# Head pairs 6 and 7 move from plain float32 to float32r split stacks and channel-major numerators

## The chip, the cores and the metric

One core of one Trainium2 chip runs the whole program. The metric is the device time of one execution in microseconds (us). A profiled execution also gives a trace: start and duration of every instruction on the five engines (PE is TensorE's matmuls, PEld its weight loads, DVE VectorE, ACT ScalarE, POOL GpSimd; SP issues most transfers).

## The reference, cut to what matters

Two stages, chained. First a feature-map attention without softmax over 8 batches, 8 heads, 576 positions, head width 64, 128 features:

```python
def phi(x):
    proj = np.einsum('bhsd,df->bhsf', x, w_phi)
    proj = proj - np.max(np.abs(proj), axis=-1, keepdims=True)
    return np.concatenate([np.exp(proj), np.exp(-proj)], axis=-1)
q_p, k_p = (phi(q), phi(k))
kv = np.einsum('bhsf,bhsd->bhfd', k_p, v)
z = np.sum(k_p, axis=2)
num = np.einsum('bhsf,bhfd->bhsd', q_p, kv)
den = np.einsum('bhsf,bhf->bhs', q_p, z)[..., None] + 1e-06
x = num / den                       # heads side by side: (8, 576, 512)
```

Then a mixer over x: token mixing `u = x + (relu(x.T @ w_tok1) @ w_tok2).T` (576 to 256 and back), and channel mixing `u + relu(u @ w_ch1) @ w_ch2` (512 to 1536 and back).

## The kernel before

Heads are worked in pairs: pair i holds heads 2p and 2p+1 of batch i // 4, so there are 32 pairs, four to a batch. Five Python generators emit the work (`weave`, L635): `keys` (L280) and `queries` (L347) walk the pairs, `token_stream` the batches in two halves of two pairs each, `load_weights` the weights, `channel_stream` the 18 blocks of 256 positions. The framework then schedules the emitted instructions on each engine's queue by a timeline of its own; every engine runs its queue in order.

**Projection** (`less_max`, L218). A plain pair (i < `PLAIN`) is loaded by `load_plain` (L269), the keys of pair i in the upper 64 partitions and the queries of pair i in the lower 64, and multiplied by `wz` (w_phi padded with zeros) as float32, one 128x128 matmul for each 128 positions: 9 for the keys, 9 for the queries. The trace has two records for each plain float32 matmul. A split pair is loaded by `load` (L262) into `raw`, and `stack` (L206) writes a rounded copy by DVE (L213) and the remainder by POOL (L214) into the two halves of a tile; one float32r matmul 256 wide then gives two partial projections, which ACT copies (L246) and DVE adds (L248). In both, DVE takes the largest absolute value (L253); the subtraction of it (L255) is on DVE for a plain pair (it reads PSUM), on POOL for a split one. ACT makes the two exponentials (L299).

**Key-value sums** (`add_kv`, L310): 18 float32 matmuls a pair into `pkv`, with 128 moving columns for i < `ROWS` and 65 behind them. For i < `ROWS` ACT copies them out once (L333); behind, ACT rounds them (L341) and DVE makes the remainder (L343).

**Numerators.** The projected queries are transposed on PE (L393) and exponentiated. For i < `ROWS`, `row_numerators` (L418) has positions in rows: 20 float32 matmuls with 65 columns (L432, 40 records), a division on DVE (L445 to L447) into `rows`, 5 transposes back (`flip`, L451). Behind them `numerators` (L463) has channels in rows: ACT makes a rounded copy (L406), DVE and POOL the remainders (L407), and 24 float32r matmuls of 256 and 320 columns follow (`pn`), with DVE transposes of the denominators (L479, L484) and a product on POOL (L486).

**Token mixing** (`token_mix`, L500) takes `rows` as they are when the half has them; otherwise it transposes `xt` on PE (`px`, L510). The remainder of its input is on POOL with `rows`, on DVE without.

**Channel mixing** (`channel_mix`, L549): six up-projections `h` of 24 matmuls a block (`up_proj`), each followed by a ReLU on ACT (`gh`, L576) and a remainder on DVE (`gl`, L577), and six down-projections into `acc`. `h` has one PSUM buffer, so the next up-projection waits until `gl` has read it. The two weight matrices of this stage arrive as 64-bit floats and are converted on the core until some 155 us: ACT (L147), four DVE instructions on 128x512 elements (L148 to L151, `bitsc`), ACT's rounding and POOL's remainder (L75, L78, `wc`).

Of the kernel before, what the change touches and what calls it, by code (L numbers as in the profile page):

```python
# [22 lines left out]
T = 256  # L23
E = 1536
NC_, NE, NT = C // P, E // P, T // P
PLAIN = 8
ROWS = 8
BURST = 8
GATES = [1, 2, 2, 3, 4, 4, 5, 6, 6, 7, 7, 7]
HELD = {15: 1, 17: 2, 19: 3, 21: 4}  # L30
# [15 lines left out]
def mixer_kernel(ctx, tc, qk, vm, vt, w_phi, w1, w2, wc1, wc2d, out):  # L46
# [159 lines left out]
    def stack(raw, base, name):  # L206

        out = []
        lo = D - base
        for k, (c, n) in enumerate(((0, 512), (512, 640))):  # L210
            t = wk.tile([P, n], F32R, tag=f"{name[0]}{k}", name=f"st{name}{k}", bufs=1)
            src = raw[base:base + D, c:c + n]
            nc.vector.tensor_copy(t[base:base + D], src)  # L213
            nc.gpsimd.tensor_tensor(t[lo:lo + D], src, t[base:base + D].bitcast(F32), op=ALU.subtract)  # L214
            out.append(t)
        return out
# [45 lines left out]
    def load(i):  # L262

        raw = wk.tile([P, 2 * S], F32, tag="raw", name=f"raw{i}", bufs=1)
        lo, hi = (D if i <= PLAIN else 0), (D if i == B * NP else P)
        nc.sync.dma_start(raw[lo:hi], qk[i, lo:hi])
        raws[i] = raw

    def load_plain(i):  # L269

        out = []
        for k, (c, n) in enumerate(((0, 512), (512, 640))):
            t = wk.tile([P, n], F32, tag=f"{'kq'[i % 2]}{k}", name=f"pair{i}{k}", bufs=1)
            nc.sync.dma_start(t[D:], qk[i, D:, c:c + n])
            out.append(t)
        for k, (c, n) in enumerate(((0, 512), (512, 640))):
            nc.sync.dma_start(out[k][:D], qk[i + 1, :D, c:c + n])
        pairs[i] = out

    def keys():  # L280
        groups = [[(0, 0), (0, 1)], [(0, 2), (0, 3)], [(1, 0), (1, 1)], [(1, 2), (1, 3)], [None]]
        todo = None
        for i in range(B * NP):
            yield from until(lambda: i < 2 or i - 2 in asked)
            if i < PLAIN:
                load_plain(i)
# [4 lines left out]
            for j in range(2):  # L291
                queue.dma_start(v_sb[j * D:(j + 1) * D, 4, j, :D], vt[i, j])
            plain = D if i < PLAIN else None
            ts = pairs[i] if i < PLAIN else stack(raws[i], D, f"k{i}")
            for g, us in enumerate(groups):
# [14 lines left out]
    def add_kv(i, g, us, kp, v_sb):  # L310
# [4 lines left out]
        for n, u in enumerate(us):  # L315
            for sg in range(2):
                if u is None:
                    o, v = pkv[:, sg], v_sb[:, 4]
                elif i < ROWS:
                    c = (2 * u[1] + u[0]) * (D + 1)  # L320
# [7 lines left out]

        if i < ROWS:
            kv = wk.tile([P, 2, 4, D], F32, tag="kv0", name=f"kv0_{i}", bufs=1)  # L330
# [16 lines left out]
    def queries():  # L347
        turned, split_up, row_major = None, None, None
        pieces = [(i, k, j) for i in range(B * NP) for k in range(2) for j in range(2)] + [None] * 3
        for piece in pieces:  # L350
# [4 lines left out]
            if split_up:  # L355
                yield from until(lambda: split_up[0] in kvs)
                if split_up[0] < ROWS:
                    row_major = row_numerators(*split_up)
# [8 lines left out]
            if piece:  # L367
                i, k, j = piece
                if (k, j) == (0, 0):
                    plain = 0 if i < PLAIN else None  # L370
                    if i < PLAIN:
                        yield from until(lambda: i in pairs)
# [13 lines left out]
    def turn(i, k, j, pm, tail):  # L386
# [11 lines left out]
        for sg in range(2):  # L398
            full = wk.tile([P, SEG[0][1]], F32, tag="qf", name=f"qf{i}_{k}{j}{sg}")[:, :w]
            nc.scalar.activation(full, src, AF.Exp, scale=1.0 - 2.0 * sg)  # L400
            if i < ROWS:
                qps.append(full)
# [15 lines left out]
    def row_numerators(i, k, j, qps):  # L418

        b, p = divmod(i, NP)
        h, p = divmod(p, 2)
        n = 3 - k
        if j == 0:
            sums[0] = ps_w.tile([P, 2, 3, D + 1], F32, **REST, name=f"pr{i}_{k}")
        pn = sums[0]
        at = (D if j == 1 else 0) if k == 0 else 0
        for u in range(n):
            w, c = (P, at + u * P) if u < 2 else (D, 0 if j == 1 else 2 * P)  # L430
            for sg in range(2):
                nc.tensor.matmul(pn[:w, j, u], qps[sg][:, c:c + w], kvs[i][:, sg, j],  # L432
                                 start=j == 0 and u == 0 and sg == 0, stop=j == 1 and u == n - 1 and sg == 1,
                                 skip_group_check=True)
        if j == 0:
            return None
        if (b, h) not in rows_of:
            rows_of[b, h] = wk.tile([P, 5, 2 * P], F32, tag="rows", name=f"rows{b}_{h}")
        x = rows_of[b, h][:, 3 * k:3 * k + n, p * P:p * P + P].rearrange("p u (j d) -> p j u d", j=2)
        den = column(wk, 8, tag="dn", name=f"dn{i}_{k}", bufs=4)  # L440
        if i < NP:
            gates.append(den[:, :1])
        for w, a, e in ((P, 0, 2), (D, 2, 3))[:2 - k]:
            d = den[:w, 2 * a:2 * e].rearrange("p (j u) -> p j u", j=2)
            nc.vector.tensor_scalar(d, pn[:w, :, a:e, D], 1e-6, None, op0=ALU.add)  # L445
            nc.vector.reciprocal(d, d)
            nc.vector.tensor_tensor(x[:w, :, a:e], pn[:w, :, a:e, :D],  # L447
                                    d.unsqueeze(3).to_broadcast([w, 2, e - a, D]), op=ALU.mult)
        return i, k
# [40 lines left out]
    def until(cond):  # L490
        while not cond():
            yield None
# [205 lines left out]
```

## Time and profile before

| | us |
|---|---|
| median of 3 runs | 1130.9 (1129.98 to 1130.96) |
| the profiled execution | 1130.58 |
| its span, first to last instruction | 1128.8 |
| PE busy in it | 1109.2 |
| DVE, ACT, POOL busy | 669.1, 542.7, 512.0 |

The span is 1.8 us below the time of its own execution. The granted TensorE clock is 0.999 over the run, so 2.4 GHz. Matmul records overlap (each is some 280 ns long while one starts about every 117 ns), so what a matmul costs is read from the spacing in the chain of work, and not from its record's length.

### The profile page before, as it was taken

How to read it: one execution, taken by the hardware profiler on the slowest of the kernel's cores; microseconds unless marked ns; L12 is line 12 of the kernel's file. 1: busy time of each engine (PE TensorE's matmuls, PEld its weight loads, DVE VectorE, ACT ScalarE, POOL GpSimd, SP SyncE). 2: the span in 40 equal slices, each digit the busy share in tenths (PEclk: the TensorE clock that was granted, in tenths of full speed). 3: DMA queues.
4: the chain of work that ended last, by engine and by line, in shares of the span. 5: the costliest groups of instructions: out<-in, count | busy, mean ns of one | idle time of the engine just before them, and what ended most of it. 6: DMA issues, size and time to landing. Idle time of an engine off the chain costs nothing.

```text
span 1128.8 us, 24388 instructions
## 1 busy us (share of the span) xinstructions
PE 1109.2 (98%) x9280; PEld 1092.9 (97%) x9280; DVE 669.1 (59%) x1655; ACT 542.7 (48%) x1589; POOL 512.0 (45%) x675
## 2 busy tenths in 40 slices
PE   8999999999999999999999999999999999999998
PEld 7998999989999999989999999999999999999998
DVE  7889864476575756677465573664756675542111
ACT  5766543445464644556454463544645565441110
POOL 2334332465464744756364472644645474330110
PEclk9999999999999999999999999999999999999999
DMA  7545401111110111111011110111101110000000
GB/s 210 169 127 163 138 16 43 32 52 33 29 54 20 33 33 51 33 51 33 20 33 51 33 51 1 52 33 38 46 19 33 51 33 12 20 1 19 20 20 20
DMA packets 66164, 54.39 MB, mean 48 GB/s; under 512 B 44992, under 2 KB 56768, under 8 KB 66048
## 3 DMA queue, kind: packets, MB, share of 16 engines
q1 hardware_dynamic: 64528, 52.41, 15.9%
q8 instruction: 74, 1.21, 0.4%
q10 hardware_dynamic: 1520, 0.43, 0.2%
q14 instruction: 42, 0.34, 0.1%
HBM read 43.38 MB, written 9.44 MB: 47 GB/s over the span
## 4 chain that ended last, share of the span: by engine, by line
PE 87%; DVE 5%; POOL 3%; ACT 2%; DMA 2%; issue 1%; SPq 0%; POOLq 0%; ACTq 0%; DVEq 0%
PE acc L84 26%; PE h L84 26%; PE pkv L324 9%; PE pn L84 6%; PE ph L84 3%; PE pa L84 3%; PE pt L393 3%; PE pr L432 2%; PE ppk L239 2%; PE ppq L239 2%; PE px L510 1%; POOL stq L214 1%; PE ppq L243 1%; PE ppk L243 1%; DMA raw<-in_w 1%
## 5 line engine op out<-in xcount | busy, mean ns | idle before, releaser
L84 PE MATMUL acc<-gh,wc 128*128 128x256 f32 x1728 | 342.6, 283 | 0.2 <-ACT gh L576 0.2
L84 PEld LDWEIGHTS acc<-gh,wc 128*128 128x128 f32 x1728 | 275.6, 188 | 0.8 <-ACT gh L576 0.7
L84 PE MATMUL h<-uh,wc_h 128*128 128x256 f32 x864 | 245.5, 285 | 0.6 <-DVE gl L577 0.5
L84 PE MATMUL h<-uh,wc_l 128*128 128x256 f32 x864 | 244.4, 283 | 0.0
L84 PE MATMUL h<-ul,wc_h 128*128 128x256 f32 x864 | 243.6, 282 | 0.8 <-POOL ul L557 0.8
L84 PE MATMUL acc<-gl,wc 128*128 128x256 f32 x864 | 241.9, 282 | 0.0
L84 PEld LDWEIGHTS h<-uh,wc_h 128*128 128x128 f32 x864 | 162.5, 188 | 2.0 <-DVE gl L577 1.6
L84 PEld LDWEIGHTS h<-ul,wc_h 128*128 128x128 f32 x864 | 162.8, 188 | 1.2 <-POOL ul L557 1.1
L84 PEld LDWEIGHTS acc<-gl,wc 128*128 128x128 f32 x864 | 162.7, 188 | 0.0
L84 PEld LDWEIGHTS h<-uh,wc_l 128*128 128x128 f32 x864 | 162.5, 188 | 0.0
L324 PE MATMUL pkv<-v,kp 128*128 128x65 f32 (+2 forms) x1152 | 156.3, 270 | 0.6 <-ACT kv L333 0.2
L299 ACT ACTIVATE kp<-pmk 128x256 f32<-128x256 f32 (+1 forms) x320 | 109.6, 393 | 94.0 <-POOL pmk L255 76.7
L577 DVE SCALAR_TENSOR_TENSOR gl<-h,gh 128x512 fp32r<-128x512 f32 x108 | 74.4, 689 | 131.0 <-ACT gh L576 127.3
L407 POOL TENSOR_TENSOR ql<-qf,qh 128x320 fp32r<-128x320 f32 (+1 forms) x96 | 80.7, 840 | 152.7 <-ACT qh L406 146.7
L400 ACT ACTIVATE qf<-pt 128x320 f32<-128x320 f32 (+1 forms) x256 | 103.7, 417 | 94.4 <-PE pt L393 76.9
L324 PEld LDWEIGHTS pkv<-v,kp 128*128 128x128 f32 x1152 | 146.1, 191 | 2.3 <-ACT kp L299 1.2
L576 ACT ACTIVATE gh<-h 128x512 fp32r<-128x512 f32 x108 | 64.8, 600 | 131.6 <-PE h L84 130.3
L557 POOL TENSOR_TENSOR ul<-xt,uh 128x64 fp32r<-128x64 f32 (+3 forms) x120 | 60.5, 531 | 95.4 <-ACT uh L556 94.6
L84 PE MATMUL pn<-qh,kv 128*128 128x320 f32 (+1 forms) x384 | 101.0, 302 | 1.8 <-DVE xs L515 1.8
L255 POOL TENSOR_TENSOR pmk<-pk,mxk 128x256 f32<-128x256 f32 (+1 forms) x120 | 71.9, 599 | 43.7 <-DVE mxk L253 23.5
L255 POOL TENSOR_TENSOR pmq<-pq,mxq 128x256 f32<-128x256 f32 x96 | 61.6, 642 | 62.8 <-DVE mxq L253 57.6
L214 POOL TENSOR_TENSOR stq<-raw,stq 64x512 fp32r<-64x512 f32 (+1 forms) x48 | 69.7, 1452 | 37.9 <-DVE stq L213 35.3
(124 smaller groups left out, 2251.6 us busy)
## 6 DMA issues: line engine op xcount, KB each, us to landing
raw<-in_qk SPq DMA_DIRECT2D x23, 576.0 KB, 3.8
rawc<-in_wc SPq DMA_DIRECT2D x24, 512.0 KB, 4.1
v<-in_vm SPq DMA_DIRECT2D x31, 256.0 KB, 3.4
out_x<-xt SPq DMA_DIRECT2D x12, 256.0 KB, 2.2
out_x<-xt SPq DMA_DIRECT2D x16, 192.0 KB, 2.0
pair<-in_qk SPq DMA_DIRECT2D x16, 160.0 KB, 4.0
pair<-in_qk SPq DMA_DIRECT2D x16, 128.0 KB, 3.8
raw<-in_w SPq DMA_DIRECT2D x8, 256.0 KB, 5.9
```

Source lines behind the costliest of these rows:

```text
L84: nc.tensor.matmul(o, a, m, start=first and i == 0, stop=last and i == 2, skip_group_check=group_ok)
L214: nc.gpsimd.tensor_tensor(t[lo:lo + D], src, t[base:base + D].bitcast(F32), op=ALU.subtract)
L239: nc.tensor.matmul(ps[:, i].rearrange("p two f -> p (two f)"), t[:, c:c + P], wp2.rearrange("p two f -> p (two f)"), start=True, stop=True)
L255: eng.tensor_tensor(pm[:, :n], pr, mx[:, :n].unsqueeze(2).to_broadcast([P, n, F]), op=ALU.subtract)
L299: nc.scalar.activation(kp[:, :len(us), sg], pm[:, :len(us)], AF.Exp, scale=1.0 - 2.0 * sg)
L324: nc.tensor.matmul(o, kp[:, n, sg], v, start=g == 0 and n == 0 and sg == 0, stop=u is None, skip_group_check=True)
L393: nc.tensor.transpose(ptr[:, n], r, ident)
L400: nc.scalar.activation(full, src, AF.Exp, scale=1.0 - 2.0 * sg)
L407: (nc.gpsimd if sg else nc.vector).tensor_tensor(lo, full, hi.bitcast(F32), op=ALU.subtract)
L557: nc.gpsimd.tensor_tensor(l[:, d:d + n], t[:, c, o:o + n], h[:, d:d + n].bitcast(F32), op=ALU.subtract)
L576: nc.scalar.activation(gh, ph, AF.Relu)
L577: nc.vector.scalar_tensor_tensor(gl, ph, 0.0, gh.bitcast(F32), op0=ALU.max, op1=ALU.subtract)
```

## The change

Two constants. `PLAIN` decides which pairs are loaded and projected as plain float32, `ROWS` which have 128-column key-value sums and row-major numerators:

```diff
-PLAIN = 8
-ROWS = 8
+PLAIN = 6
+ROWS = 6
```

Pairs 6 and 7 are the second half of batch 1, so token mixing of that half takes the `px` transposes. The emitted order changes with it. Three places show how.

On PE, where the keys of pair 6 are projected (`ppk`; `pf` are the transposes back of pair 5, `pkv` its key-value sums, `h_0` channel mixing's first up-projection), a piece of the difference:

```order
 L84 MATMUL ph_1_1_1_1523<-w_h,al_1_1437 128x256
-L243 MATMUL ppk_0_1555<-wz,pair_1546 128x128 x2
+L84 MATMUL h_0_1589<-uh_2_1579,wc_h 128x256
+L239 MATMUL ppk_0_1557<-wp_89,stk_1551 128x256 x2
 L324 MATMUL pkv_1331<-v_111,kp_4_1503 128x2x65 x2
-L84 MATMUL h_0_1583<-ul_2_1574,wc_h 128x256
-L84 MATMUL h_0_1583<-uh_2_1573,wc_l 128x256
-L84 MATMUL h_0_1583<-uh_3_1577,wc_h 128x256
+L84 MATMUL h_0_1589<-ul_2_1580,wc_h 128x256
+L84 MATMUL h_0_1589<-uh_2_1579,wc_l 128x256
+L84 MATMUL h_0_1589<-uh_3_1583,wc_h 128x256
 L458 MATMUL pf_0_1467<-ident,rows_0_1406 128x128 x2
```

The projection keeps its place; two float32 matmuls (four records) became two float32r ones (two records).

On DVE, around the first remainder `gl_0` of channel mixing (`bitsc` are weight conversions, `rows` and `dn` the numerators of pair 4):

```order
+L248 TENSOR_TENSOR pk_0_1562<-ppk_0_1557,partk_0_1560 128x256
 L446 RECIPROCAL dn_0_1407<-dn_0_1407 64x2
-L255 TENSOR_TENSOR pmk_0_1560<-ppk_0_1555,mxk_0_1558 128x256
 L149 TENSOR_SCALAR bitsc_6_1372<-bitsc_6_1372 128x512
 L151 SCALAR_TENSOR_TENSOR bitsc_5_1339<-rawc_5_1337,bitsc_5_1339 128x512
+L253 TENSOR_REDUCE mxk_0_1564<-pk_0_1562 128x2
 L447 TENSOR_TENSOR rows_0_1406<-pr_0_1293,dn_0_1407 64x128
-L577 SCALAR_TENSOR_TENSOR gl_0_1609<-h_0_1583,gh_0_1608 128x512
 L150 SCALAR_TENSOR_TENSOR bitsc_6_1372<-rawc_6_1370,bitsc_6_1372 128x512
-L253 TENSOR_REDUCE mxk_1_1697<-ppk_1_1694 128x2
+L577 SCALAR_TENSOR_TENSOR gl_0_1615<-h_0_1589,gh_0_1614 128x512
```

The additions of pair 6 stand between the same conversions, its subtractions are gone from here, and the remainder stands one conversion later.

On POOL, in the same stretch (`stk_15..` is the stack of pair 6, `stk_2066` the first of pair 7, `wc` the weight remainders):

```order
 L78 TENSOR_TENSOR wc_l<-bitsc_1_512_1209,wc_h 128x512
+L214 TENSOR_TENSOR stk_1551<-raw_1546,stk_1551 64x512
 L78 TENSOR_TENSOR wc_l<-bitsc_2_512_1220,wc_h 128x512
 L78 TENSOR_TENSOR wc_l<-bitsc_3_512_1262,wc_h 128x512
-L557 TENSOR_TENSOR ul_2_1574<-xt_0_397,uh_2_1573 128x256
-L557 TENSOR_TENSOR ul_3_1578<-xt_0_397,uh_3_1577 128x256
+L557 TENSOR_TENSOR ul_2_1580<-xt_0_397,uh_2_1579 128x256
+L557 TENSOR_TENSOR ul_3_1584<-xt_0_397,uh_3_1583 128x256
+L214 TENSOR_TENSOR stk_1554<-raw_1546,stk_1554 64x640
 L78 TENSOR_TENSOR wc_4_1300<-bitsc_4_1303,wc_4_1300 128x512
+L255 TENSOR_TENSOR pmk_0_1566<-pk_0_1562,mxk_0_1564 128x256
 L78 TENSOR_TENSOR wc_5_1336<-bitsc_5_1339,wc_5_1336 128x512
```

The stack remainders and the subtractions of pair 6 now stand among the weight remainders.

## Rows read from the trace of the kernel before

**Rows 1.** The page: busy time, share of the span, instructions of each engine
```profile
PE 1109.2 (98%) x9280; PEld 1092.9 (97%) x9280; DVE 669.1 (59%) x1655; ACT 542.7 (48%) x1589; POOL 512.0 (45%) x675
```
**Rows 2.** Windows: length, busy us of PE, PEld, DVE, ACT, POOL, clock, DMA
```profile
82.00:121.00 39.00, 37.01 (x301) 34.85 (x301) 38.01 (x86) 23.99 (x57) 17.71 (x18) 1.00 0.51 151
121.00:156.00 35.00, 35.00 (x302) 34.35 (x303) 27.35 (x63) 19.21 (x47) 11.79 (x10) 1.00 0.26 87
82.00:151.00 69.00, 67.01 (x559) 64.39 (x560) 62.53 (x142) 40.63 (x95) 28.36 (x27) 1.00 0.42 129
```
**Rows 3.** Timeline of DVE and of PE: second and fifth remainder, next up-projection
```profile
120.24 0.68 DVE L577 SCALAR_TENSOR_TENSOR gl<-h,gh 128x512 fp32r<-128x512 f32 x1
120.98 0.39 PE L84 MATMUL h<-uh,wc_h 128*128 128x256 f32 x1
150.43 0.68 DVE L577 SCALAR_TENSOR_TENSOR gl<-h,gh 128x512 fp32r<-128x512 f32 x1
153.66 0.28 PE L84 MATMUL h<-uh,wc_h 128*128 128x256 f32 x1
```
**Rows 4.** The chain that ended last, in time: start, us, what, how many records
```profile
122.55 1.21 PE pr L432 x12
130.43 0.45 PE ppk L243 x4
131.33 0.89 PE pkv L324 x8
174.95 0.42 PE pf L458 x3
...
286.23 0.22 PE px L510 x2
430.77 0.88 PE pn L84 x6
439.62 0.47 PE pn L84 x4
```
**Rows 5.** Groups by shape, whole run: count, busy us, mean ns, idle before
```profile
L213 DVE CAST stk<-raw 64x640 fp32r<-64x640 f32 x24 | 14.3, 598 | 10.0 <-PE ppk L239 9.4
L213 DVE CAST stk<-raw 64x512 fp32r<-64x512 f32 x24 | 12.8, 534 | 12.2 <-DMA raw<-in_qk 8.8 <-PE ppk L239 2.8
L255 DVE TENSOR_TENSOR pmk<-ppk,mxk 128x256 f32<-128x256 f32 x32 | 13.1, 411 | 0.3
L214 POOL TENSOR_TENSOR stk<-raw,stk 64x640 fp32r<-64x640 f32 x24 | 37.4, 1558 | 16.3 <-DVE stk L213 16.0
L214 POOL TENSOR_TENSOR stk<-raw,stk 64x512 fp32r<-64x512 f32 x24 | 31.0, 1290 | 15.9 <-DVE stk L213 10.0 <-POOL ql L407 2.9 <-POOL pmq L255 1.7
L255 POOL TENSOR_TENSOR pmk<-pk,mxk 128x256 f32<-128x256 f32 x96 | 62.3, 649 | 39.9 <-DVE mxk L253 23.5 <-PE h L84 7.9 <-PE pkv L324 3.1
```
**Rows 6.** Timeline of DVE and of POOL: conversions alone and beside POOL
```profile
108.32 0.41 DVE L149 TENSOR_SCALAR bitsc<-bitsc 128x512 uint32<-128x512 uint32 x1
115.70 0.68 DVE L151 SCALAR_TENSOR_TENSOR bitsc<-rawc,bitsc 128x512 uint32<-128x512 uint32 x1
117.14 1.51 DVE L149 TENSOR_SCALAR bitsc<-bitsc 128x512 uint32<-128x512 uint32 x1
117.10 1.27 POOL L78 TENSOR_TENSOR wc<-bitsc,wc 128x512 fp32r<-128x512 f32 x1 [2.41 <-ACT wc L75]
```
**Rows 7.** Groups by shape of DVE, 82 to 121 us: count, busy us, mean ns
```profile
L151 DVE SCALAR_TENSOR_TENSOR bitsc<-rawc,bitsc 128x512 uint32<-128x512 uint32 x10 | 8.0, 802 | 0.1
L150 DVE SCALAR_TENSOR_TENSOR bitsc<-rawc,bitsc 128x512 uint32<-128x512 uint32 x10 | 7.8, 789 | 0.0
L149 DVE TENSOR_SCALAR bitsc<-bitsc 128x512 uint32<-128x512 uint32 x9 | 6.0, 671 | 0.1
L148 DVE TENSOR_SCALAR bitsc<-bitsc 128x512 f32<-128x512 f32 x9 | 5.2, 578 | 0.4 <-ACT bitsc L147 0.4
```
**Rows 8.** Window in which token mixing of batch 1 meets the next pairs
```profile
226.00:254.00 28.00, 26.10 (x204) 24.48 (x203) 20.15 (x48) 13.76 (x44) 17.29 (x21) 1.00 0.19 52
```

## The prediction

> **What bounds the kernel now.** I read the page first: PE is busy 98% of the span, no engine beside it and its weight loads over 59% [rows 1]. That is a mean, so I read windows next. From 82 to 121 us DVE is busy 38.0 of 39.0 us and PE 37.0; from 121 to 156 PE is busy all 35 us and DVE 27.4 [rows 2]. So there are two regimes: up to some 121 us DVE and PE are both full (DVE converts the channel weights there), behind it PE alone sets the pace and a matmul less is time less, if its inputs come in time. The timeline shows where one regime hands over: the second remainder of channel mixing ends on DVE at 120.9 us, and the up-projection that needs its PSUM buffer starts at 120.98; at the fifth the remainder ends at 151.1 and the sixth up-projection starts at 153.66, 2.6 us later [rows 3]. The pairs that change are worked just here, between 104 and some 220 us, half of them where DVE has no room.
>
> **What PE loses.** Prices are spacings in the chain [rows 4]; one plain float32 matmul is two records. Projections of a pair: before 18 matmuls, 36 records at 0.45/4 = 0.1125 us, 4.05 us; after 18 records of 256 columns, as the numerators' 256-column ones at 0.47/4 = 0.118, 2.12 us. Saved 1.93. Numerators: before 40 records at 1.21/12 = 0.101 and 5 transposes back at 0.42/3 = 0.14, together 4.74 us; after 12 of 320 columns at 0.88/6 = 0.147, 12 of 256 at 0.118 and 5 `px` transposes at 0.22/2 = 0.11, together 3.72. Saved 1.02. The key-value sums keep 36 records; 128 columns go at 0.89/8 = 0.111, the 65-column row I have nearest is the numerators' 0.101, so at most 0.36 us, and I count nothing, since both seem set by the weight load that each record has. Sum 2.95 us a pair, **5.9 us for two** (6.6 with the key-value sums).
>
> **What DVE gets before the hand-over.** I follow it to the fifth remainder, `gl_4`, and count in the order of both kernels. Ahead of it stand six casts for three stacks (keys of 6, queries of 6, keys of 7) and seven additions that are new, and nine subtractions that are gone. Casts 3 x (0.598 + 0.534) = 3.4 us; seven additions less nine subtractions, all at about 0.41, -0.8 [rows 5]. So 2.6 us more work of its own. The maximum stays.
>
> **What POOL adds, and what that does to DVE.** Ahead of the same point POOL gets six stack remainders, 3 x (1.558 + 1.290) = 8.5 us, and seven subtractions at 0.649, 4.5 us: 13.1 us [rows 5]. POOL has the time: 17.7 of 39.0 us before 121, 11.8 of 35 behind it [rows 2]. But it slows DVE: a conversion step that takes 0.41 us alone took 1.51 when a POOL subtraction of 1.27 us began 0.04 us ahead of it [rows 6]. The mean price: in 82 to 121 us the four steps average 0.578, 0.671, 0.789 and 0.802 [rows 7], against 0.41 for the first two and 0.68 for the others alone (I take the one step of each length that [rows 6] has), so 9 x 0.17 + 9 x 0.26 + 10 x 0.11 + 10 x 0.12 = 6.2 us lost, for 17.7 us of POOL: 0.35 us a POOL microsecond. The bounds are nothing (POOL works while DVE reads PSUM) and 1 (each POOL instruction blocks a step entirely). Of the 13.1 us, 5.4 stand ahead of the second remainder (two stack remainders of pair 6, one of pair 7, two subtractions): 1.9 us. For the other 7.7 I take two thirds of the price, since DVE is then busy 78% and not 97% [rows 2] and fewer conversions are left: 1.8 us. Together 3.7.
>
> The Trainium skill's page "SBUF — State Buffer", section "Who interferes with whom", speaks against this change: a DVE instruction in a two-port mode or with two SBUF inputs and a GpSimd instruction that reads SBUF hold one port pair in turn, and the later one is blocked for the whole instruction. The trace agrees for the single step of [rows 6]; over all steps the mean is a third of that. By the rule for every step the sum would be 1137.8 us, by the mean price 1128.5.
>
> **The sum.** DVE's room from 82 to 151 us is 69.0 - 62.5 = 6.5 us [rows 2]. At the 97.5% that it reached before 121 only 4.7 of them can be used; I take 6.0, nearer the upper end, because most of the idle time lies behind 121, where DVE waits for others that would now be ready. `gl_4` then ends at 151.1 + 2.6 + 3.7 - 6.0 = 151.4 us and the sixth up-projection starts at 151.5, which is 2.2 us earlier than 153.7. PE itself could be there 6.0 us earlier: in the new order there are ahead of it 18 plain projections fewer (-4.05) and 16 float32r ones more (+1.89), 4 key-value matmuls fewer (8 records, -0.89), 6 of the query transposes (-0.66), 6 row numerators (12 records, -1.21), 2 transposes back (-0.28), 9 of token mixing (-1.06), and 2 of the down-projection more (+0.24). PE thus waits some 3.8 us in all for DVE on the way. Behind this point PE's work is as before (-5.9 + 6.0), and DVE has ample room, so what is won by 151.5 stays: 2.2 - 0.1 = **2.1 us**. From the profiled execution's 1130.58 (span and 1.8 us around it) that is **1128.5 us**. The median of the runs is 0.3 above that execution.
>
> **Costed at nothing.** ACT's copies of partial projections and its second exponentials: ACT is busy 24.0 of 39.0 and 19.2 of 35.0 us [rows 2]; without that cover, each `part` copy would hold the addition, and so the transposes of its piece. The load of pair 7 now waits on SP until POOL has read pair 6's `raw`, and six weight loads are queued behind it; DMA is busy 0.51 [rows 2] and these loads wait for their own buffers there anyway. If that cover fails, conversions come late and the wait moves to the up-projection. DVE's and POOL's larger load for the numerators of 6 and 7 (`ql`, transposes, products) falls behind 151 us, where PE is full and channel mixing fills in.
>
> **The rivals.**
> *PE keeps nearly all of it.* With the price of POOL at nothing and all 6.5 us of room, `gl_4` ends at 147.2 and PE's own 6.0 us is the limit: gain 5.9, 1124.7 (1124.0 with the key-value sums). For it: the up-projections wait for a remainder only at a few places, and in 121 to 156 PE is full. Against it: it needs DVE without a pause.
> *All is swallowed.* Price 0.35 throughout (4.6 us) and 4.7 us of room: `gl_4` at 153.6, the sixth up-projection as late as before, 1130.6. For it: DVE at 97% beside the new work. Against it: 2.6 us of slack behind the fifth remainder.
> *Slower, by the port.* Every POOL microsecond costs DVE a whole one: 151.1 + 2.6 + 13.1 - 6.0 = 160.8 us, 7.1 us later than before, 1137.8. It decides from a price of 0.46 on (151.1 + 2.6 + 6.0 - 6.0 = 153.7), and passes 0.2% at 0.65. For it: the single step, and that stack remainders of 1.3 to 1.6 us are as long as the weight remainders that blocked it. Against it: the mean of 17.7 us of the same kind is 0.35. This is what the rule of the Trainium skill's page "SBUF — State Buffer" would give if every step met it.
> *A wider hole at token mixing.* From 226 to 254 us PE is idle 1.9 us, where the second half of batch 1 is mixed [rows 8]; with `px` transposes in front, its input is one step later. A second such hole takes the 2.1 back: 1130.4.
>
> **How the numbers follow.** Chances: the part-swallowed case (gain 0.8 to 4) 0.40, nearly all kept 0.24, all swallowed 0.18, the wider hole 0.06, slower by the port 0.12. The measurement tells 0.2%, 2.3 us, from no change, so faster means under 1128.6 by the median. The first case straddles that: half of it and the second case make 0.45 faster; the port case and a tail of the hole make 0.16 slower; 0.39 the same. The range reaches from the second case's end with the key-value sums, 1124.0, up into the port case, to 1133.0 (a price of 0.64); it leaves out most of that case and little below.
>
> **What would show it.** Right: PE busy 6 us less in sum; in the new trace DVE over 95% busy from 82 to some 150 us, conversions averaging longer than the 0.67 and 0.80 of before, the sixth up-projection starting within 0.2 us of the fifth remainder's end, near 151.5 us. Wrong in the first term: `ppk` pieces of 256 columns spaced over 0.13 us. Wrong in the second: the sixth up-projection starts near 147.7, well behind its remainder, so that DVE never bound. The prediction fails upward if conversions average over 1 us, or if PE waits for POOL's weight remainders, which now stand behind the stacks.

## The result and the profile after

| | us | against before, 95% interval |
|---|---|---|
| before | 1130.74 (1129.98 to 1130.96) | |
| changed | 1142.61 (1141.95 to 1143.19) | 1.0102 [1.009, 1.0115] |
| its profiled execution, span | 1142.69, 1140.8 | |

The change makes the kernel 11.9 us slower, outside the range of the prediction. The page of the changed kernel, its busy times and the row of the granted clock (40 slices of 28.5 us, in tenths):

```profile
PE 1113.5 (98%) x9212; PEld 1096.1 (96%) x9212; DVE 693.0 (61%) x1683; ACT 557.0 (49%) x1633; POOL 545.8 (48%) x711
PEclk9999989999999999999999999999999999999999
```

PE has 68 records less than in [rows 1] and is busy 4.3 us longer; one slice of the clock has an 8. So I read the windows around it. The changed kernel (columns as in [rows 2]; the clock is third from the end):

```profile
82.00:121.00 39.00, 34.37 (x249) 32.15 (x250) 37.81 (x78) 22.08 (x53) 22.49 (x22) 0.91 0.47 138
121.00:156.00 35.00, 32.28 (x272) 31.04 (x270) 30.96 (x61) 16.72 (x38) 18.77 (x15) 1.00 0.32 100
...
82.00:160.94 78.94, 69.47 (x527) 65.13 (x527) 73.65 (x146) 42.34 (x102) 42.64 (x38) 0.92 0.38 113
152.00:156.00 4.00, 2.00 (x15) 1.58 (x13) 3.97 (x7) 1.28 (x2) 2.66 (x3) 0.99 0.47 147
156.00:160.00 4.00, 2.44 (x8) 1.84 (x8) 3.93 (x7) 3.02 (x10) 1.38 (x2) 0.50 0.04 8
160.00:164.00 4.00, 3.40 (x16) 3.10 (x16) 3.46 (x9) 0.89 (x2) 2.53 (x4) 0.50 0.01 3
164.00:168.00 4.00, 4.00 (x28) 4.00 (x28) 1.59 (x4) 2.81 (x11) 3.92 (x7) 0.73 0.00 0
240.00:268.00 28.00, 26.61 (x212) 25.25 (x211) 21.24 (x54) 16.59 (x50) 18.75 (x24) 1.00 0.12 33
```

In 82 to 121 us PE is busy 34.4 us at a mean clock of 0.91 (it is 0.50 from 105 to 108 us and again from 115 to 118), against 37.0 at 1.00 [rows 2], and POOL 22.5 against 17.7. From 152 us DVE is full, PE is busy half the time, and then its clock is 0.50, which is 1.2 GHz in place of 2.4. The chain of waits of the changed kernel shows what that makes of the hand-over, and what the new matmuls cost:

```profile
160.26 0.69 DVE gl L577
160.99 5.39 PE h L84 x24
...
174.50 0.23 PE ppk L239 x2
...
182.03 0.88 PE pn L84 x6
...
232.83 0.22 PE px L510 x2
```

The fifth remainder ends at 160.94 (before 151.11 [rows 3]), the sixth up-projection starts at 160.99 (153.66), and its 24 matmuls take 5.39 us where 24 at full clock take 2.8. DVE's timeline ahead of that point, then POOL's:

```profile
151.19 2.05 DVE L151 SCALAR_TENSOR_TENSOR bitsc<-rawc,bitsc 128x512 uint32<-128x512 uint32 x1
...
157.03 0.43 DVE L149 TENSOR_SCALAR bitsc<-bitsc 128x512 uint32<-128x512 uint32 x1
157.49 1.71 DVE L150 SCALAR_TENSOR_TENSOR bitsc<-rawc,bitsc 128x512 uint32<-128x512 uint32 x1
159.13 0.41 DVE L248 TENSOR_TENSOR pk<-ppk,partk 128x256 f32<-128x256 f32 x1
...
159.66 0.67 DVE L151 SCALAR_TENSOR_TENSOR bitsc<-rawc,bitsc 128x512 uint32<-128x512 uint32 x1
160.26 0.68 DVE L577 SCALAR_TENSOR_TENSOR gl<-h,gh 128x512 fp32r<-128x512 f32 x1
```
```profile
150.97 1.73 POOL L214 TENSOR_TENSOR stk<-raw,stk 64x640 fp32r<-64x640 f32 x1 [3.10 <-DVE stk L213]
...
157.39 1.27 POOL L78 TENSOR_TENSOR wc<-bitsc,wc 128x512 fp32r<-128x512 f32 x1 [1.27 <-ACT wc L75]
```

A step of 0.68 us takes 2.05 beside a stack remainder of pair 7, and the last conversion's L149 to L151 stand ahead of the fifth remainder. In the kernel before they stand behind it:

```profile
150.43 0.68 DVE L577 SCALAR_TENSOR_TENSOR gl<-h,gh 128x512 fp32r<-128x512 f32 x1
151.03 0.41 DVE L149 TENSOR_SCALAR bitsc<-bitsc 128x512 uint32<-128x512 uint32 x1
...
151.80 0.68 DVE L150 SCALAR_TENSOR_TENSOR bitsc<-rawc,bitsc 128x512 uint32<-128x512 uint32 x1
...
152.73 0.68 DVE L151 SCALAR_TENSOR_TENSOR bitsc<-rawc,bitsc 128x512 uint32<-128x512 uint32 x1
```

All conversion steps from 82 to 161 us, grouped (count, busy us, mean ns), before:

```profile
L151 DVE SCALAR_TENSOR_TENSOR bitsc<-rawc,bitsc 128x512 uint32<-128x512 uint32 x17 | 13.6, 810 | 0.1
L150 DVE SCALAR_TENSOR_TENSOR bitsc<-rawc,bitsc 128x512 uint32<-128x512 uint32 x17 | 12.4, 745 | 0.0
L149 DVE TENSOR_SCALAR bitsc<-bitsc 128x512 uint32<-128x512 uint32 x16 | 9.6, 607 | 0.1
L148 DVE TENSOR_SCALAR bitsc<-bitsc 128x512 f32<-128x512 f32 x15 | 8.6, 573 | 2.2 <-ACT bitsc L147 2.2
```

and after:

```profile
L151 DVE SCALAR_TENSOR_TENSOR bitsc<-rawc,bitsc 128x512 uint32<-128x512 uint32 x17 | 16.0, 940 | 0.2
L150 DVE SCALAR_TENSOR_TENSOR bitsc<-rawc,bitsc 128x512 uint32<-128x512 uint32 x17 | 14.9, 882 | 0.1
L149 DVE TENSOR_SCALAR bitsc<-bitsc 128x512 uint32<-128x512 uint32 x16 | 10.6, 664 | 0.2
L148 DVE TENSOR_SCALAR bitsc<-bitsc 128x512 f32<-128x512 f32 x15 | 10.4, 696 | 1.4 <-ACT bitsc L147 1.2
```

The same 65 steps keep DVE busy 51.9 us, not 44.2: 7.7 us of stretch. The prediction's signs were partly there: conversions average longer, under 1 us, and DVE is busy 73.65 of 78.94 us up to the fifth remainder, 93% and not over 95.

### The profile page after: what moved, and what is told of

It reads as the page before. It is cut to its first block, busy times and chain, and to the rows that moved or that the text cites. A ratio compares the mean times of both kernels' runs of the same rounds, so it can differ in the third digit from the quotient of the medians.

```text
span 1140.8 us, 24389 instructions
## 1 busy us (share of the span) xinstructions
PE 1113.5 (98%) x9212; PEld 1096.1 (96%) x9212; DVE 693.0 (61%) x1683; ACT 557.0 (49%) x1633; POOL 545.8 (48%) x711
## 4 chain that ended last, share of the span: by engine, by line
PE 85%; DVE 7%; POOL 3%; ACT 2%; issue 2%; DMA 1%; ACTq 0%; SPq 0%; POOLq 0%; DVEq 0%
PE acc L84 25%; PE h L84 25%; PE pkv L324 9%; PE pn L84 7%; PE ph L84 4%; PE pa L84 3%; PE pt L393 3%; PE ppk L239 2%; PE ppq L239 2%; PE pr L432 1%; PE px L510 1%; DVE bitsc L150 1%; POOL stq L214 1%; DVE bitsc L151 1%; DVE bitsc L148 1%
## 5 line engine op out<-in xcount | busy, mean ns | idle before, releaser
L84 PE MATMUL h<-uh,wc_h 128*128 128x256 f32 x864 | 248.0, 287 | 1.3 <-DVE gl L577 1.1
L407 POOL TENSOR_TENSOR ql<-qf,qh 128x320 fp32r<-128x320 f32 (+1 forms) x104 | 87.4, 840 | 168.9 <-ACT qh L406 162.6
L84 PE MATMUL pn<-qh,kv 128*128 128x320 f32 (+1 forms) x416 | 109.6, 302 | 2.0 <-DVE xs L515 2.0
L255 POOL TENSOR_TENSOR pmk<-pk,mxk 128x256 f32<-128x256 f32 (+1 forms) x130 | 80.9, 622 | 42.0 <-DVE mxk L253 24.2
L255 POOL TENSOR_TENSOR pmq<-pq,mxq 128x256 f32<-128x256 f32 x104 | 66.6, 641 | 66.2 <-DVE mxq L253 60.0
L214 POOL TENSOR_TENSOR stq<-raw,stq 64x512 fp32r<-64x512 f32 (+1 forms) x52 | 75.5, 1452 | 32.9 <-DVE stq L213 29.4
```

Of the source, the lines that this page charges most:

```text
L84: nc.tensor.matmul(o, a, m, start=first and i == 0, stop=last and i == 2, skip_group_check=group_ok)
L255: eng.tensor_tensor(pm[:, :n], pr, mx[:, :n].unsqueeze(2).to_broadcast([P, n, F]), op=ALU.subtract)
L407: (nc.gpsimd if sg else nc.vector).tensor_tensor(lo, full, hi.bitcast(F32), op=ALU.subtract)
```

## The experiments

The theory: POOL's new work and DVE's own delay the fifth remainder where DVE is full with conversions, PE idles, and its clock falls. Rivals: the numerators or the transposes cost; the longer chain over ACT, DVE and POOL costs by itself; the clock's fall costs nothing, since PE waits for DVE anyway.

**One half of the change each.** e1 has the first of these edits of the kernel before, e2 the second:

```diff
-PLAIN = 8
+PLAIN = 6
```
```diff
-ROWS = 8
+ROWS = 6
```

> Only the projections of pairs 6 and 7 change; their key-value sums and numerators stay row-major. Theory (POOL's stack remainders and subtractions slow the conversions on DVE, and the late remainder lets PE idle and its clock fall): all of it is in here, so 9 to 14 us slower than before, 1140 to 1145 us, with the sixth up-projection near 160 us and a stretch of clock 0.5 behind it. Rival (the numerators and the transposes of token mixing are what costs): near before less the 3.9 us of the projections, 1126 to 1130.

> Only the key-value sums and numerators of pairs 6 and 7 change; the projections stay plain, so no stack and no subtraction of theirs is on POOL. Theory: the conversions keep their lengths, the sixth up-projection starts at 153 to 154 us as before, and the saving of the numerators, 1.0 to 1.4 us a pair, stays: 1127.5 to 1129.5 us. Rival (numerators and transposes cost): over 1135.

Measured: e1 1146.20 us (1.0136 [1.0121, 1.0151]), e2 1126.95 (0.9966 [0.9953, 0.9979]). The loss of 15.2 and the gain of 4.1 add up to 11.1, near the 11.9 of the whole. All the loss is in the projections: in e1 the fifth remainder ends at 160.03 and the clock is 0.50 from 156 to 164 us. In e2 it ends at 152.01, PE is busy all of 152 to 172, and this version beats both kernels.

**POOL's share, taken away.** e3 is the changed kernel with this edit, where `EARLY` names the stacks of pairs 6 and 7; their lower half is then a second copy, and the kernel leaves the remainder out:

```diff
-            nc.gpsimd.tensor_tensor(t[lo:lo + D], src, t[base:base + D].bitcast(F32), op=ALU.subtract)
+            if name in EARLY:
+                nc.scalar.copy(t[lo:lo + D], src)
+            else:
+                nc.gpsimd.tensor_tensor(t[lo:lo + D], src, t[base:base + D].bitcast(F32), op=ALU.subtract)
```

e5 has also, for their subtractions of the maximum,

```diff
-            pr, eng = pr[:, :n], nc.gpsimd
+            pr, eng = pr[:, :n], nc.vector if name.split('_')[0][1:] in ('6', '7') else nc.gpsimd
```

> The changed kernel, but the lower half of the stacks of pairs 6 and 7 is a plain ACT copy in place of POOL's remainder (the output loses precision there). It takes 8.5 us of POOL from the stretch ahead of the fifth remainder and gives ACT some 6. Theory: the fifth remainder ends 4 to 8 us earlier than 160.9, the clock does not fall, and the time is 1128 to 1135. Rival (not the port, but DVE's own new work and the longer chain of copy, addition, subtraction over three engines): the remainder is late as before, 1140 to 1145.

> As e3_rem_on_act, and the subtractions of pairs 6 and 7 are on DVE in place of POOL: nothing that the change gave POOL ahead of the fifth remainder is left there. Of the 11.6 us of loss e3 gave back 3.8. Theory (POOL beside the conversions, and what waits in its queue): each subtraction on DVE costs 0.41 us and frees 0.65 to 1.5 of POOL, and the exponentials no longer wait behind a weight remainder, so the fifth remainder ends 1 to 4 us earlier than e3's 156.1, time 1132 to 1137. Rival (DVE's own work is what counts, POOL little): seven more DVE instructions make it 2 to 3 us later, 1140 to 1142.

e3: 1138.82 us (1.0071 [1.0056, 1.0086]), the fifth remainder ends at 156.07, 4.9 us earlier than in the changed kernel. The time missed the expected range, for the clock fell here too. e5: 1135.51 (1.0040 [1.0025, 1.0055]), as expected, but its fifth remainder ends at 156.02, by the trace's time no earlier than in e3. That trace, however, is late before anything that was edited. The DVE step `xs` of token mixing starts at 85.36 us in the kernel before, at 85.70 in the changed one, and so in e3 and in e5:

```profile
85.26 0.42 DVE L519 TENSOR_TENSOR xs<-rows,xs 64x256 fp32r<-64x256 f32 x1
86.63 0.42 DVE L519 TENSOR_TENSOR xs<-rows,xs 64x256 fp32r<-64x256 f32 x1
```

From the start of this step to the end of the fifth remainder the kernel before takes 65.8 us, the changed one 75.2, e3 70.8 and e5 69.4. So POOL's stacks were worth 4.4 of the 9.5 us of delay, its subtractions 1.4 net of their time on DVE (1 to 4 were expected), and 3.6 stay without either. What goes is the stretch: held against 0.41 and 0.68 us for a step alone, the conversions between these two points are 8.2 us longer in the kernel before, 15.4 in the changed one, 11.5 in e3 and 8.1 in e5. Without POOL's new work the conversions are as they were before; e5's steps with two inputs, 82 to 161 us (L151 and L152 there are L150 and L151 elsewhere):

```profile
L152 DVE SCALAR_TENSOR_TENSOR bitsc<-rawc,bitsc 128x512 uint32<-128x512 uint32 x17 | 14.1, 829 | 0.1
L151 DVE SCALAR_TENSOR_TENSOR bitsc<-rawc,bitsc 128x512 uint32<-128x512 uint32 x17 | 12.7, 750 | 0.1
```

Behind the remainder e3 and e5 differ in the clock, here in this order:

```profile
156.00:160.00 4.00, 3.88 (x18) 3.88 (x19) 3.40 (x10) 0.62 (x3) 3.50 (x4) 0.50 0.00 0
160.00:164.00 4.00, 4.00 (x30) 4.00 (x30) 0.69 (x1) 3.35 (x12) 3.92 (x10) 0.79 0.02 4
```
```profile
156.00:160.00 4.00, 3.93 (x22) 3.93 (x23) 3.90 (x11) 0.99 (x4) 2.49 (x3) 0.64 0.00 0
160.00:164.00 4.00, 4.00 (x35) 4.00 (x35) 1.14 (x2) 2.56 (x9) 4.00 (x8) 0.94 0.02 4
```

PE is as busy and does 57 records in e5 where it does 48 in e3. From the sixth up-projection to the end of the execution e3 takes 1.2 us more (981.7 against 980.5).

**The loads alone, on the kernel before.** Work on pairs 6 and 7 that nobody reads: e6 eight POOL subtractions (the first line), e14 eight DVE copies (the second), e15 both.

```diff
+            nc.gpsimd.tensor_tensor(spare[0][base:base + D, c:c + n], src, src, op=ALU.subtract)
+            nc.vector.tensor_copy(spare[0][base:base + D, c:c + n], src)
```

> The kernel before with eight POOL subtractions of stack size (64x512 and 64x640, pairs 6 and 7) into a tile that nobody reads, and nothing else. Theory: POOL's time alone costs DVE 0.35 to 1 us for each of the 8.5 us ahead of the fifth remainder, 3 to 8.5 us, of which up to 2.6 is slack: 1131 to 1138, 1134 the middle. Rival (the port price is small, the loss is the chain): within 1 us of before, 1130 to 1132.

> The kernel before with eight DVE copies of stack size (pairs 6 and 7, all ahead of the fifth remainder) into a tile that nobody reads: 3.6 to 4.5 us of DVE work, none on POOL. Theory (DVE's idle time ahead of the fifth remainder is waiting in order and takes up little new work): the remainder ends 2.5 to 4.5 us later than 151.1, of which 2.6 is slack at the sixth up-projection, so 1130.5 to 1133. Rival (the room of 6.5 us is there, as the prediction had it): the remainder within 1 us of 151.1, the time within 1 us of before, or under it.

> The kernel before with both idle loads, the eight DVE copies of e14 and the eight POOL subtractions of e6, and PE's work unchanged. Theory (load on DVE and POOL alone makes the loss): the shifts of e6 (5.1 us) and e14 add up, the fifth remainder ends at 158 to 161, the clock falls behind it, 1138 to 1146. Rival (part of the loss needs the longer chain of the split projection over ACT, DVE and POOL): as e6 alone, 1135 to 1139.

| | us, ratio | fifth remainder ends | later by | later, counted from `xs` | conversions longer by (from `xs`, as above) |
|---|---|---|---|---|---|
| e6, POOL | 1137.89, 1.0068 [1.0052, 1.0085] | 156.18 | 5.1 | 5.8 | 2.4 |
| e14, DVE | 1140.38, 1.0083 [1.0066, 1.0100] | 155.41 | 4.3 | 4.1 | -0.9 |
| e15, both | 1145.46, 1.0126 [1.0111, 1.0141] | 164.35 | 13.2 | 12.9 | 7.5 |

All eight POOL instructions of e6 came to stand ahead of the fifth remainder (the expectation counted six). From `xs` on POOL is busy 11.7 us more than in the kernel before, and the remainder is 5.8 us later, but that is no price of 0.5 for the port. The conversions are only 2.4 us longer, 0.2 for a POOL microsecond; 1.1 us is two more conversion steps that now stand ahead of the remainder, and DVE is idle 2.5 us longer. Most of its idle time stands ahead of three of the remainders, which the trace shows waiting for POOL's weight remainders. In the kernel before two of them wait, and less long:

```profile
130.04 0.69 DVE L577 SCALAR_TENSOR_TENSOR gl<-h,gh 128x512 fp32r<-128x512 f32 x1 [1.26 <-POOL wc_l L78]
140.89 0.69 DVE L577 SCALAR_TENSOR_TENSOR gl<-h,gh 128x512 fp32r<-128x512 f32 x1 [1.47 <-POOL wc L78]
```

The kernel fits that: `gl`, `gh` and the conversions' `bits` take turns in four buffers of one tag, so `gl` can have to wait until POOL has read one of them. (e6's trace is of its fastest execution, 1134.82 us.) The timeline shows how POOL acts on a single step, DVE first:

```profile
106.90 0.41 DVE L265 TENSOR_TENSOR pmq<-ppq,mxq 128x256 f32<-128x256 f32 x1
107.23 0.40 DVE L263 TENSOR_REDUCE mxk<-ppk 128x2 f32<-128x256 f32 x1
107.56 0.56 DVE L148 TENSOR_SCALAR bitsc<-bitsc 128x512 f32<-128x512 f32 x1
108.04 1.79 DVE L150 SCALAR_TENSOR_TENSOR bitsc<-rawc,bitsc 128x512 uint32<-128x512 uint32 x1
```
```profile
106.59 2.64 POOL L226 TENSOR_TENSOR spare<-pair 64x640 f32<-64x640 f32 x2
```

The two steps that read PSUM keep their 0.41 and 0.40 us beside POOL; the conversion, which reads two tiles of SBUF, takes 1.79 instead of 0.68. That fits the Trainium skill's page "SBUF — State Buffer", section "Who interferes with whom": it is instructions with two SBUF inputs (beside a GpSimd instruction that reads SBUF, as here), or in a two-port mode, that share a port with GpSimd.

In e14 the copies themselves take 5.4 us and delay the remainder by 4.1, counted from `xs`. DVE is idle 5.75 us there, 6.44 in the kernel before, so only 0.7 us went into its idle time; the conversions are 0.9 us shorter. Its copies, grouped from 82 to 161 us:

```profile
L226 DVE COPY spare<-pair 64x640 f32<-64x640 f32 x4 | 3.7, 926 | 0.1
L226 DVE COPY spare<-pair 64x512 f32<-64x512 f32 x4 | 1.7, 418 | 1.3 <-DMA pair<-in_qk 1.3
```

The time of e14 was expected at 1133 at most. It is 7 us over that: the sixth up-projection starts 3.0 us later than before, and 6.6 us more go behind it. The clock fell in two places (0.88 in 112 to 126 us, 0.79 in 244 to 252), each time behind a stretch in which PE had waited (10.2 of 14 us busy in 98 to 112, 6.2 of 8 in 236 to 244), but the second fall is worth 1.7 us only. PE has also 2.4 us more work left there, at the prices of [rows 4]; the other 2.5 stay open.

e15's remainder was expected at 158 to 161 us. It is later, since the two loads do more than add up: beside each other the copies take 7.5 us and the conversions are 7.5 us longer. So the same POOL instructions cost 0.2 of their time in e6 and 0.6 here. The clock did not fall behind the remainder, as expected, but ahead of it (0.86 in 140 to 152). e15 reaches the loss of the change and more with PE's work and the chain over the engines as before; so that chain is not needed for the loss.

**The clock alone.** The changed kernel with float32r matmuls of 256 columns into a spare PSUM buffer, where PE is idle: e7 with 20 and 17, and 8 float32 ones at 101 us; e11 with 36 and 8, late only. The two lines that both share (`x` is an earlier remainder `gl`):

```diff
+        for at in range(n):
+            nc.tensor.matmul(o, wp2[:, 0], x, start=at == 0, stop=at == n - 1)
```

> The changed kernel with matmuls that nobody reads where PE waits: 8 float32 ones of 124 columns near 101 us, 20 and 17 float32r ones of 256 columns (4.4 us at full clock) between the fourth down-projection and the sixth up-projection. They depend on nothing late and change nothing for the other engines. Theory (the clock's fall to 0.5 at 104 and at 156 us is a cost of its own): the clock stays at 1.00 and the 24 matmuls of the sixth up-projection take 2.8 us, not 5.4, so the time falls by 3 to 5 us, to 1137.5 to 1139.5. Rival (the fall only goes with the waits and costs nothing, since PE then waits for DVE anyway): 1142 to 1147, the dummies are a net cost.

> The changed kernel with 36 and 8 float32r matmuls of 256 columns that nobody reads, all between the third quarter of the fourth down-projection and the sixth up-projection, where PE of the changed kernel is idle some 5 of 9 us; nothing near 101 us this time, and none behind the wait at the first projection of pair 7 but eight. Theory (the fall of the clock has its own price): no stretch of 0.5 from 156 to 166, the 24 matmuls of the sixth up-projection in 2.8 us, time 1138 to 1140.5. Rival (no price of its own): 1142 to 1145.

e7 1141.05 us (1.0090 [1.0073, 1.0107]), e11 1142.30 (1.0104 [1.0089, 1.0119]): by the time alone the theory missed, and e11's time lies in the rival's range. In e7 the early ones moved the first fall, to 114 to 121 us, and behind a wait of 1.9 us for a projection of pair 7 a second came at 162. In e11 the late fall is gone:

```profile
156.00:160.00 4.00, 3.26 (x25) 3.05 (x26) 3.93 (x8) 2.10 (x7) 1.30 (x1) 1.00 0.04 8
160.00:164.00 4.00, 3.03 (x23) 2.55 (x21) 3.78 (x10) 1.80 (x6) 3.42 (x4) 1.00 0.00 0
164.00:168.00 4.00, 3.91 (x34) 3.92 (x34) 0.42 (x3) 2.43 (x10) 2.76 (x7) 1.00 0.02 4
```

but with the dummies the framework ordered the queues anew. Ahead of the fifth remainder stand now eight DVE instructions (additions of projections, maxima, a cast, the remainder of key-value sums) that stood behind it, and it ends at 164.03, 3.1 us later. What the clock costs is read from the sixth up-projection's start to the end: 1142.02 - 164.09 = 977.9 us in e11, 1142.69 - 160.99 = 981.7 in the changed kernel, 1130.58 - 153.66 = 976.9 before. e11 takes 3.8 us less than the changed kernel. Of these, 1.1 are work that PE has already done by then in e11 (eight records of key-value sums, two of projections, at the prices of [rows 4]). The other 2.7 fit the late fall: behind 160.99 the clock is at 0.50 for 5.1 us more, half of which is 2.6 (an estimate).

**Less DVE work.** The clamp of the conversion (L148) left out: e8 and e9 everywhere, on the kernel before and the changed one; e12 and e13 for the channel weights only.

```diff
-        nc.vector.tensor_scalar(m.bitcast(F32), m.bitcast(F32), LEAST, MOST, op0=ALU.max, op1=ALU.min)
```

> The kernel before without the clamp in the weight conversion, the DVE step of L148 (a weight under 2 to the power of -15 or over 122880 would be converted wrongly). It takes 15 steps, 8.6 us, off DVE between 82 and 161 us. Base line for e9. Theory and rival alike: DVE is full up to 121 us there, so the first remainder comes earlier and the time falls by 2 to 6 us, to 1125 to 1129.

> The changed kernel without the same clamp. Theory (the change loses only because its work meets a DVE that is full with conversions): with some 10 us of room the loss against e8 shrinks from 11.6 to under 6 us, 1127 to 1133. Rival (the longer chain over ACT, DVE and POOL, or something behind 170 us, costs by itself): the loss against e8 stays 10 to 12 us, 1136 to 1140.

> As e8_before_noclamp, but the clamp is left out for the channel weights only, so that the start of the program, where a late load cost e8 some 6 us at 32 us, stays as it is. DVE loses 15 steps, 8.6 us, from 82 to 161 us. Base line for e13: 1125 to 1130.

> The changed kernel with the same clamp left out for the channel weights only. Theory (the change loses because its work meets a DVE full with conversions): the loss against e12 is under half of 11.6 us, or a gain. Rival (longer chain over three engines, or a cost behind 170 us): it stays at 10 to 12 us.

| | on before | on the changed kernel |
|---|---|---|
| everywhere | e8 1139.55, 1.0073 [1.0051, 1.0095] | e9 1132.46, 1.0016 [1.0004, 1.0027] |
| channel weights | e12 1135.73, 1.0042 [1.0025, 1.0059] | e13 1130.79, 1.0000 [0.9991, 1.0009] |

e8's chain has a wait for a load early on, which spoils it as a base line (e9's has one of 6.82 us, so those two can be held against each other):

```profile
31.75 6.58 DMA pair<-in_qk
```

e12 and e13 have nothing of that. With the clamp gone the changed kernel gains 11.8 us: in e13 the fifth remainder ends at 153.04, the clock, 0.50 from 101 to 108 us, stays at 1.00 from 112 on, and PE is busy 1104.1 us, 5.1 under [rows 1]. The loss against e12 turned into a gain of 4.9. Both base lines missed: a kernel with less DVE work is slower than before. In e12 the fifth remainder comes little later than it did (152.26), but a hole at token mixing grew, and the clock fell in it:

```profile
236.00:240.00 4.00, 2.04 (x13) 1.62 (x13) 2.33 (x5) 2.28 (x8) 3.84 (x5) 0.94 0.00 0
240.00:244.00 4.00, 3.49 (x15) 3.49 (x16) 2.68 (x7) 1.37 (x4) 1.89 (x3) 0.50 0.29 66
```

Some 3.4 of the 4.9 us are that fall (an estimate: half of 239.5 to 246.3 us, where the clock is at 0.50). Why the hole grew is open.

**Where the border lies.** e10 and e16, again edits of the kernel before:

```diff
-PLAIN = 8
-ROWS = 8
+PLAIN = 7
+ROWS = 6
```
```diff
-ROWS = 8
+ROWS = 4
```

> Only pair 7 gets the split projections; both pairs get the new numerators (1126.95 us in e2_num_only, which keeps both projections plain). Theory: pair 7's first stack remainder stands at 117 us and the second at 151 us, its queries behind the conversions, so it adds two of the six stack remainders ahead of the fifth remainder (2.8 of 8.5 us) and no subtraction: 1 to 5 us over e2, 1128 to 1132, less the 1.9 us that its projections save. Rival (any split pair in this stretch costs the whole 7 us and the fall of the clock): 1134 to 1139.

> The version that gained (plain projections up to pair 7, e2_num_only, 1126.95 us) with the new numerators from pair 4 on. Those of pairs 4 and 5 fall between 95 and 160 us. Theory (DVE and POOL beside the conversions are what is short): their remainders on POOL (ql, two pairs) and DVE's remainders and transposes make the first half later, 1129 to 1140, over e2. Rival (numerators are cheap wherever they stand): 1.0 to 1.4 us a pair less than e2, 1124 to 1125.

e10: 1129.10 us (0.9986 [0.9976, 0.9995]), so of the 15.7 us between e2 and the change pair 7 costs 2.2 and pair 6 the other 13.5. e16: 1136.92 (1.0052 [1.0037, 1.0067]), 10 us over e2; its first remainder ends at 120.62 (before 110.12), its clock is 0.76 in 98 to 112. The numerators lose as the projections do where they meet the conversions.

## Why the prediction was wrong

**PE's term was right.** Two split pieces take 0.23 us, six numerators 0.88, two transposes 0.22, as [rows 4] had them. e2 gains 4.1 us where 2.0 to 2.8 were counted for numerators and key-value sums (its interval begins at 2.4). e13 has 5.1 of the 5.9 in PE's busy time.

**DVE's own work: 2.6 by luck.** Casts took 3.1 us and additions 2.6, and nine subtractions are gone (-3.4), all near what was counted. Four maxima that now stand behind the fifth remainder (-1.5) were overlooked, and so were the three steps of the last conversion that now stand ahead of it (0.41 + 0.68 + 0.68 = 1.8). The sum is 2.6 again.

**POOL's effect was mis-sized: 3.7 forecast, 7.7 measured.** Of POOL's new work from 82 to 161 us the six stack remainders take 8.8 us, as counted; of subtractions five stand there, not seven, and take 5.4 (those of 128x256 a mean of 1.13 us in place of 0.65: they stretch too). 7.7 for 14.2 us is a price of 0.54. I took 0.35, a mean over POOL work that partly stood beside steps that read PSUM, and two thirds of it behind 121 us. The miss lies there. By the lengths of single steps (7.3 us in sum, since busy time counts overlaps once) 2.5 us of stretch stand ahead of the second remainder, where 1.9 were forecast, and 4.8 behind it, where 1.8 were. L151 in 121 to 161 us:

```profile
L151 DVE SCALAR_TENSOR_TENSOR bitsc<-rawc,bitsc 128x512 uint32<-128x512 uint32 x9 | 8.9, 988 | 0.1
```

My reading, which no run shows by itself, is that what is added there follows DVE's casts directly, among conversions. That the price is no constant is shown: 0.2 in e6, 0.6 in e15.

**The room is the step that failed: 6.0 forecast, 1.2 measured.** "I take 6.0, nearer the upper end, because most of the idle time lies behind 121, where DVE waits for others that would now be ready." They were not. From 82 us to the fifth remainder DVE was idle 6.5 us before and is idle 78.94 - 73.65 = 5.3 after. e14 took up 0.7 of 5.4 us of copies, and e5, without POOL's new work, 2.9 of 6.5. DVE runs its queue in order; its idle time is waits, in the trace before for POOL's weight remainders (2.8 us), for ACT (2.2) and for PE (1.0), and in the one after for ACT (3.0), POOL (0.7) and PE (0.4). They did not shrink by what was added.

With the measured terms: 151.1 + 2.6 + 7.7 - 1.2 = 160.2, 0.7 short of the measured 160.9. Of these, 0.3 are there before the new work begins (`xs` at 85.70 and 85.36); I take the rest for other steps that are longer beside POOL.

**Behind the hand-over nothing was counted, and 4.8 us were lost.** "Behind this point [...] what is won by 151.5 stays" may hold for a gain. On the way to a sixth up-projection that is 7.3 us late PE was idle, and the clock fell to 1.2 GHz; the 5.1 us that it stayed there behind the hand-over cost 2.6 more. The profiled executions differ by 12.1 us: 7.3 + 2.6, and 2.2 that I can't place.

**The rivals.** "Slower, by the port" named the place and 160.8 us for the fifth remainder. It had the sum right with two terms wrong: a price of 1 with 6.0 us of room, where it is 0.54 with 1.2. Its time fell 4.8 us short, 2.6 of them for want of the clock. The wider hole at token mixing did not come: PE is busy 26.6 of 28 us there, against 26.1 [rows 8]. PE did not wait for weights whose remainders came late; it did wait 1.8 us for exponentials (ACT's `kp`) whose subtraction stood behind a weight remainder in POOL's queue.

## What to carry to other kernels

Idle time of an engine that runs its queue in order is room only if what it waits for comes earlier too; without a row that shows that, count none of it. Price work on a second engine by the steps that it will stand beside, not by the mean over what it stood beside before (0.2 to 0.6 for the same POOL instructions here). Compare two traces from a step that no edit touches, since one can be late by a microsecond from its start. And recount in the new order every instruction ahead of the point that decides. Where an engine is already full, a delay is followed by a hole on PE and then by its clock, so keep conversions and extra stages apart: the half of this change that lies behind the conversions is worth 4.1 us on its own.

## What the hardware showed that was not expected

The granted clock fell to 0.50 behind holes of PE and stayed there while PE was busy again. In the changed kernel PE is idle from 102 to 104 us, where it waits for DVE's `xt`, and the clock is 0.50 from 105 to 108. From 111 to 114 us PE is busy 0.58 to 0.78 of each microsecond, and the clock is 0.50 from 115 to 118, with PE busy all the time:

```profile
115.00:116.00 1.00, 1.00 (x7) 1.00 (x6) 1.00 (x1) 1.00 (x4) 0.68 (x1) 0.50 0.83 332
```

The third time it is 0.50 from 156 to 166 us, during the last 5 of which PE never stopped. In the kernel before, PE's holes at 100 to 104 us leave 0.53 to 0.82 of each microsecond busy, and the clock stays at 1.00. The Trainium skill's page "TensorE: Matmul & The Clock Gate", section "Part 1: The HAM clock gate (the "warmup" mystery)", has it that the low clock is the resting state and activity releases it; the rows agree. That eight DVE copies of 5.4 us cost 9 us, and that leaving out 8.6 us of DVE work made the kernel before 5 us slower, both come with such falls, which account for 1.7 us behind the hand-over in the first and some 3.4 in the second.
